# Attention, gated MoE and a second feed-forward on one core: another filler for TensorE and fewer weight conversions at the start

## The chip, the core and the metric

The kernel runs on one core of a Trainium2 chip. The core has a matrix engine (TensorE, PE in the profile, with its weight loads as PEld), three elementwise engines (VectorE or DVE, ScalarE or ACT, GpSimd or POOL) and SyncE (SP), which issues DMA transfers here. Each engine takes its instructions in program order, and semaphores join them. The metric is device time in microseconds (us) of one execution; the clock of TensorE can be granted at 1.2 or at 2.4 GHz.

## What is computed

Three layers follow one another, all in 32-bit floats:

```python
# attention: batch 4, 8 heads, 576 positions, head width 64
scores = q @ k.T / 8 + minimum(cum[j] - cum[i], 0)     # causal, cum = cumsum(max(s, 0))
x = softmax(scores) @ v                                # gathered to 2304 x 512
# gated layer, 512 -> 1536 -> 512
x = (sigmoid(x @ w_gate) * (x @ w_val)) @ w_out
# second layer, 512 -> 2048 -> 512
h = x @ w_in
out = (h - tanh(h)) @ w_out2
```

The weights reach the kernel as 64-bit words (doubles), and the kernel itself turns each block of them into 32-bit floats, and these into a high part (fp32r) and a low part, so that a product of the gated layer is three passes: high times high, low times high, high times low.

## The kernel before

The program is one stream of work per engine, written out in order. Attention runs as steps `i`, one for each pair of a head and a block of 128 query rows. The first 16 heads ("units" `u` below `N32`) do their rows 0 to 255 in two steps each, plain 32-bit products with a contraction of 65 rows; later units use split operands. Steps 0 to 31 are those of the first kind, from step 32 on come the others.

A step issues, in this order: the scaled scores' reduction on DVE (`ttr`, L391), for the step two back the reciprocal of its row sum on DVE and its normalisation on POOL (`norm`, L414), the evacuation of transposes on ACT (`evac`, L441), the exponential on ACT (`exp`, L398), the evacuation of products of the gated layer (`moe_post`, L539 and L542), loads on SP, then on PE the next step's scores (`qk`, L363 and L364), a product group of the gated layer (`moe`, L526 to L530) if one is queued, the transposes of the step two back (`tr`, L428), and at the end of a head the product with the values (`pv`, L459). PE takes them in that order: a transpose that waits for its `norm` holds everything behind it.

Products of the gated layer can start when a batch's x is whole, that is after the eighth head: the first is issued at step 20. Until then (`i < 2 * H + 4`, that is 20 steps) each step issues one idle product, `warm(1)`: a 128x128 identity against 512 columns of zeros (L588). Ahead of the first scores stand `WARM = 9` of the same. All idle products write bank 0, and each waits for the one before.

The conversion of the gated layer's 24 weight blocks is the class `Conversion`. One `tick` moves three blocks on by a stage: ACT writes the high part of block `ticks - 2` (L124), POOL its low part (L114), in `cut` pieces that `low` hands out one at a time, DVE joins the words of block `ticks - 1` (two instructions, L82 and L83), and ACT scales the words of block `ticks` (L78), for which its raw words must have come by DMA. `PRE` ticks stand ahead of step 0; then a step for which `CONV_AT(i)` holds ends with one tick. At the head of a step `cvt.finish` makes further ticks where the products of the step need a block that isn't done. Two ticks before the loop, five by step 14 (`CS`), and one at the end of each step from 15 on: twelve before step 20. After that one tick a step is enough until step 28, whose head forces one more. Nine steps from step 20 on have two product groups each, the next six have one.

The next batch's products start at step 36, and from there PE has work behind work until the end of the program.

## Time and profile before

| | us |
|---|---|
| median of three runs | 1082.97 |
| lowest, highest | 1082.9, 1084.63 |
| profiled execution | 1082.91 |
| its span, first to last instruction | 1080.9 |
| PE busy in the span | 1049.8 (97%) |

The span is read first, then the 40 slices: PE stands at 9 tenths or more in nearly all of them, and the slices under 9 lie in the first 110 us. A timeline of that part by engine then shows who holds PE there, the table of stretches shows the busy time and granted clock of each part, and the durations of one kind of product tell the clock's level where the table has no record of it.

### The profile page before, as it was taken

Reading aid. Unit: us, or ns where it says so; the run is one execution under the profiler, and the core shown is the slowest. Engines: PE = TensorE matmul, PEld = TensorE weight load, DVE = VectorE, ACT = ScalarE, POOL = GpSimd, SP = SyncE. Lnnn points to the kernel's source line nnn. Section 1 sums busy time; section 2 is a strip of 40 time slices with the busy share of each in tenths; the row PEclk is TensorE's granted clock in tenths of the full one; section 3 lists DMA queues with packets and bytes.
Section 4 is the critical chain, followed back from the end, with each engine's and each line's share of the span. In section 5 each row is a group of like instructions: output and inputs, shape, how many; then the busy total and the mean of one; then the engine's idle time right before and its main releaser. Section 6 shows DMA issues by size and latency. Waiting matters only on the chain.

```text
span 1080.9 us, 21941 instructions
## 1 busy us (share of the span) xinstructions
PE 1049.8 (97%) x7589; PEld 1018.6 (94%) x7589; DVE 660.8 (61%) x1627; ACT 546.3 (51%) x1288; POOL 464.7 (43%) x612
## 2 busy tenths in 40 slices
PE   8898999999999999999999999999999999999998
PEld 4697999899999999999999999999999999999997
DVE  6765565778677777664545562254444446778876
ACT  6765565667566566653434543344444433333433
POOL 4757454667556666642401220033323412354442
PEclk9898999999999999999999999999999999999999
DMA  7663346657565565515565553245457589535433
GB/s 224 211 224 99 118 133 165 198 153 172 139 181 134 161 169 160 131 42 170 174 200 174 188 157 95 77 134 167 136 200 268 203 285 336 190 106 152 138 96 100
DMA packets 119791, 177.25 MB, mean 164 GB/s; under 512 B 16960, under 2 KB 98368, under 8 KB 118400
## 3 DMA queue, kind: packets, MB, share of 16 engines
q1 hardware_dynamic: 119680, 175.85, 53.4%
q8 instruction: 60, 0.98, 0.4%
q14 instruction: 51, 0.42, 0.1%
HBM read 128.79 MB, written 47.00 MB: 163 GB/s over the span
## 4 chain that ended last, share of the span: by engine, by line
PE 88%; DVE 3%; ACT 2%; DMA 2%; issue 2%; POOL 2%; SPq 0%; DVEq 0%; POOLq 0%; ACTq 0%
PE bank L526 9%; PE bank L527 9%; PE bank L530 9%; PE bank L813 6%; PE bank L816 6%; PE bank L812 6%; PE bank L948 5%; PE bank L947 5%; PE bank L946 5%; PE bank L774 5%; PE bank L467 5%; PE bank L778 5%; PE bank L775 5%; PE bank L428 4%; PE bank L372 2%
## 5 line engine op out<-in xcount | busy, mean ns | idle before, releaser
L948 PE MATMUL bank<-wo,sl 128*128 128x256 f32 x504 | 142.6, 283 | 1.1 <-DVE sl L861 0.8
L946 PE MATMUL bank<-wo,sh 128*128 128x256 f32 x504 | 141.8, 281 | 0.1
L947 PE MATMUL bank<-wo,sh 128*128 128x256 f32 x504 | 141.7, 281 | 0.0
L812 PE MATMUL bank<-yh,big 128*128 128x288 f32 x512 | 139.6, 294 | 0.0
L813 PE MATMUL bank<-yh,big 128*128 128x288 f32 x512 | 139.6, 295 | 0.0
L446 ACT ACTIVATE pth<-bank 128x512 fp32r<-128x512 f32 (+2 forms) x128 | 59.5, 465 | 144.8 <-PE bank L467 86.2
L819 DVE TENSOR_TENSOR th<-bank,th 128x288 f32<-128x288 f32 x128 | 57.5, 456 | 114.1 <-ACT th L818 112.4
L447 DVE TENSOR_TENSOR ptl<-bank,pth 128x512 fp32r<-128x512 f32 (+2 forms) x128 | 66.7, 521 | 67.7 <-PE bank L467 37.5
L818 ACT ACTIVATE th<-bank 128x288 f32<-128x288 f32 x128 | 51.9, 410 | 101.1 <-PE bank L816 98.5
L948 PEld LDWEIGHTS bank<-wo,sl 128*128 128x128 f32 x504 | 95.3, 189 | 2.1 <-DVE sl L861 1.0
L398 ACT ACTIVATE sp<-sp,nm 128x576 f32<-128x576 f32 (+2 forms) x160 | 95.5, 597 | 2.0 <-DVE nm L391 1.8
L813 PEld LDWEIGHTS bank<-yh,big 128*128 128x128 f32 x512 | 96.1, 188 | 0.0
L812 PEld LDWEIGHTS bank<-yh,big 128*128 128x128 f32 x512 | 96.0, 188 | 0.0
L428 PE MATMUL bank<-ident,sp 128*128 128x128 f32 (+1 forms) x480 | 75.2, 265 | 21.0 <-POOL sp L414 10.8
L946 PEld LDWEIGHTS bank<-wo,sh 128*128 128x128 f32 x504 | 95.3, 189 | 0.3 <-ACT sh L859 0.3
L947 PEld LDWEIGHTS bank<-wo,sh 128*128 128x128 f32 x504 | 95.3, 189 | 0.0
L856 POOL TENSOR_TENSOR s<-g 128x256 f32<-128x256 f32 (+1 forms) x40 | 35.4, 885 | 127.3 <-DMA g<-h 97.4
L816 PE MATMUL bank<-yl,big 128*128 128x288 f32 x512 | 88.6, 294 | 0.0
L720 DVE TENSOR_TENSOR gl<-g,gh 128x384 fp32r<-128x384 f32 x72 | 39.9, 557 | 75.9 <-PE bank L778 47.6
L428 PEld LDWEIGHTS bank<-ident,sp 128*128 128x128 f32 (+1 forms) x480 | 51.9, 140 | 35.9 <-POOL sp L414 20.2
L414 POOL TENSOR_SCALAR sp<-sp,r 128x512 f32<-128x512 f32 (+1 forms) x96 | 61.4, 640 | 48.1 <-DVE r L407 35.2
L719 ACT ACTIVATE gh<-g 128x384 fp32r<-128x384 f32 x72 | 37.3, 529 | 80.7 <-PE bank L775 74.8
(374 smaller groups left out, 3210.8 us busy)
## 6 DMA issues: line engine op xcount, KB each, us to landing
h<-th SPq DMA_DIRECT2D x128, 144.0 KB, 1.9
kq<-in_kq SPq DMA_DIRECT2D x32, 448.0 KB, 3.9
raw<-in_wo SPq DMA_DIRECT2D x28, 512.0 KB, 5.0
g<-g SPq DMA_DIRECT2D x72, 192.0 KB, 2.6
g<-h SPq DMA_DIRECT2D x72, 128.0 KB, 2.2
w<-wst SPq DMA_DIRECT2D x5, 1792.0 KB, 6.2
wo<-w SPq DMA_DIRECT2D x5, 1792.0 KB, 9.1
cbc<-cum SPq DMA_DIRECT2D x32, 256.0 KB, 5.5
```

Of the source, the lines that this page charges most:

```text
L398: ACT.activation(out=e["sp"], in_=e["sp"], func=AF.Exp, scale=-1.0, bias=e["m"], accum_out=e["sum"])
L428: PE.transpose(ps[:, j, :], e["sp"][p0:128, c:c + 128], ident[p0:128, p0:128])
L447: DVE.tensor_tensor(out=pl[:, js, o:o + n], in0=e["tr"], in1=ph[:, js, o:o + n].bitcast(F), op=ALU.subtract)
L526: PE.matmul(ps, wh[:, c], xh[:, k], start=(k == 0), stop=False)
L527: PE.matmul(ps, wl[:, c], xh[:, k], start=False, stop=False)
L530: PE.matmul(ps, wh[:, c], xl[:, k], start=False, stop=(k == KD - 1))
L812: PE.matmul(ps, wh[:, c], Y_[blk][k][0], start=(k == 0), stop=False)
L813: PE.matmul(ps, wl[:, c], Y_[blk][k][0], start=False, stop=False)
L816: PE.matmul(ps, wh[:, c], Y_[blk][k][1], start=False, stop=(k == KD - 1))
L946: PE.matmul(o, sh[:, g, c], w[:, 0, f], start=(p == 0 and t == 0), stop=False)
L947: PE.matmul(o, sh[:, g, c], w[:, 1, f], start=False, stop=False)
L948: PE.matmul(o, sl[:, g, c], w[:, 0, f], start=False, stop=(p == MP - 1 and t == nt - 1))
```

## The change

- The idle products take other data: `some`, 128 rows by 256 columns in bf16, made from a running sum of 0.37 (a memset and a scan on DVE, one conversion on ACT), both as weights (its first 128 columns) and as moving data. They have 256 columns in place of 512. Twenty stand ahead of the first scores in place of nine, two stand in each step in place of one.
- One conversion tick ahead of step 0 in place of two; then ticks after steps 0, 3, 6, 10, 14, and one a step from 18 on, in place of 1, 4, 7, 10, 13 and one a step from 15 on. Eight ticks stand before step 20 in place of twelve.
- From step 19 on the low part of a block is one POOL instruction of 512 columns in place of two of 256.
- The DMA of the second block's raw words is issued ahead of the first two of v.

```diff
-WARM = 9
-PRE = 2
-CS = (1, 4, 7, 10, 13)
+WARM = 20
+PRE = 1
+CS = (0, 3, 6, 10, 14)
 def CONV_AT(i):
-    return i in CS or i > 14
+    return i in CS or i > 17
...
+    some = consts[:, 1024:1152].bitcast(BF)
     DVE.memset(zt, 0.0)
+    DVE.memset(consts[:, 512:768], 0.37)
+    DVE.tensor_tensor_scan(out=consts[:, 768:1024], data0=consts[:, 512:768], data1=consts[:, 512:768], initial=0.0,
+                           op0=ALU.add, op1=ALU.add)
+    ACT.activation(out=some, in_=consts[:, 768:1024], func=AF.Copy)
...
+    cvt.load(2)
     load_vc(0)
     load_vc(1)
-    cvt.load(2)
...
-            PE.matmul(bank(0, [128, 512]), identb, zero.bitcast(BF), start=True, stop=True)
+            PE.matmul(bank(0, [128, 256]), some[:, 0:128], some, start=True, stop=True)
...
-            warm(1)
+            warm(2)
...
+        if i == 2 * H + 3:
+            cvt.cut = 1
         if CONV_AT(i):
             cvt.tick()
```

On ACT, at the start of the program, before. The scalings of raw words (`raw`) are ticks, the two rows on `sp` are the exponentials of steps 0 and 1:

```order
L567 ACT_TABLE_LOAD
L567 ACTIVATE consts<-ident 128x128
L568 ACTIVATE consts<-consts 128x128
L78 ACTIVATE tmp<-raw 128x512
L78 ACTIVATE tmp<-raw 128x512
L398 ACTIVATE sp,sum<-sp,nm 128x128
```

And after:

```order
L565 ACT_TABLE_LOAD
L565 ACTIVATE consts<-consts 128x256
L572 ACTIVATE consts<-ident 128x128
L573 ACTIVATE consts<-consts 128x128
L78 ACTIVATE tmp<-raw 128x512
L398 ACTIVATE sp,sum<-sp,nm 128x128
L78 ACTIVATE tmp<-raw 128x512
```

The second block's scaling now stands behind the first exponential, and one conversion to bf16 (`consts<-consts 128x256`, the filler) stands ahead of all.

On ACT from the exponential of step 23 to that of step 24, before (`th` evacuates a product group, each `w..h` is the high part of one block):

```order
L398 ACTIVATE sp_939,sum<-sp_939,nm 128x256
L539 ACTIVATE th<-bank_900 128x256
L480 ACTIVATE xh<-bank_915 64x256
L124 ACTIVATE w16h<-tmp 128x512
L78 ACTIVATE tmp<-raw 128x512
L441 ACTIVATE p_947<-bank_973 128x256
L398 ACTIVATE sp,sum<-sp,nm 128x128
```

And after:

```order
L398 ACTIVATE sp_965,sum<-sp_965,nm 128x256
L539 ACTIVATE th<-bank_926 128x256
L480 ACTIVATE xh<-bank_941 64x256
L124 ACTIVATE w14h<-tmp 128x512
L78 ACTIVATE tmp<-raw 128x512
L124 ACTIVATE w05h<-tmp 128x512
L78 ACTIVATE tmp<-raw 128x512
L441 ACTIVATE p_972<-bank_998 128x256
L398 ACTIVATE sp,sum<-sp,nm 128x128
```

Two ticks stand one behind the other there, and so they do at five steps, 24 to 28; before, that is so at step 28 alone.

On POOL at steps 28 to 31, before (`kl` and `qs` split the operands of later units, `sp<-sp,r` is the normalisation for which a transpose on PE waits):

```order
L319 TENSOR_TENSOR kl<-kq,kh 128x256
L323 TENSOR_TENSOR qs<-kq,qs 64x256
L114 TENSOR_TENSOR w19l<-tmp,w19h 128x256
L414 TENSOR_SCALAR sp<-sp,r 128x256
L114 TENSOR_TENSOR w19l<-tmp,w19h 128x256
L114 TENSOR_TENSOR w010l<-tmp,w010h 128x256
L414 TENSOR_SCALAR sp<-sp,r 128x128
L114 TENSOR_TENSOR w010l<-tmp,w010h 128x256
```

And after:

```order
L319 TENSOR_TENSOR kl<-kq,kh 128x256
L323 TENSOR_TENSOR qs<-kq,qs 64x256
L114 TENSOR_TENSOR w19l<-tmp,w19h 128x512
L414 TENSOR_SCALAR sp<-sp,r 128x256
L114 TENSOR_TENSOR w010l<-tmp,w010h 128x512
L414 TENSOR_SCALAR sp<-sp,r 128x128
```

Each low part is one instruction, and it stands whole ahead of the next normalisation.

## Rows read from the trace of the kernel before

**Rows 1.** The page: PE's busy time, share and instructions.
```profile
PE 1049.8 (97%) x7589; PEld 1018.6 (94%) x7589; DVE 660.8 (61%) x1627; ACT 546.3 (51%) x1288; POOL 464.7 (43%) x612
```

**Rows 2.** Stretches: us, busy us (instructions) of PE PEld DVE ACT POOL, PEclk, DMA.
```profile
32.00:41.00 9.00, 5.60 (x33) 3.94 (x34) 8.06 (x23) 7.49 (x21) 7.72 (x11) 1.00 0.94 304
41.00:49.00 8.00, 7.58 (x35) 6.37 (x34) 4.78 (x18) 5.50 (x15) 6.03 (x10) 0.57 0.80 252
49.00:80.00 31.00, 31.00 (x251) 30.16 (x250) 21.42 (x62) 20.66 (x57) 17.39 (x26) 1.00 0.63 200
80.00:103.00 23.00, 17.82 (x124) 16.34 (x123) 13.14 (x52) 14.03 (x46) 18.65 (x33) 0.93 0.38 103
```

**Rows 3.** Timeline of PE at the start: start us, us, engine, line, operation.
```profile
2.39 5.73 PE L588 MATMUL bank<-consts 128*128 128x512 bf16 x9 [2.39 <-ACT consts L567]
7.91 0.63 PE L363 MATMUL bank<-kq 65*128 65x128 f32 x2
13.35 0.47 PE L428 MATMUL bank<-ident,sp 128*128 128x128 f32 x1 [0.86 <-POOL sp L414]
17.79 0.39 PE L363 MATMUL bank<-kq 65*128 65x128 f32 x2
```

**Rows 4.** Timeline of the other engines at the start.
```profile
0.91 0.54 DVE L560 MEMSET zt<- 32x576 f32 x1 [0.91 <-PEq L988]
2.67 0.28 DVE L570 TENSOR_SCALAR sraw<-sraw 32x256 f32<-32x256 f32 x1 [1.22 <-DMA sraw<-in_s]
2.99 0.68 DVE L571 TENSOR_TENSOR_SCAN cumsum<-sraw,zt 32x256 f32<-32x256 f32 x1
10.07 0.66 ACT L78 ACTIVATE tmp<-raw 128x512 f32<-128x512 f32 x1 [4.37 <-DMA raw<-in_wv]
10.63 0.39 ACT L398 ACTIVATE sp<-sp,nm 128x128 f32<-128x128 f32 x1
```

**Rows 5.** Timeline of PE: scores issued at steps 7, 15 and 19.
```profile
20.30 0.39 PE L363 MATMUL bank<-kq 65*128 65x128 f32 x2
...
32.81 0.39 PE L363 MATMUL bank<-kq 65*128 65x128 f32 x2
...
41.43 0.49 PE L363 MATMUL bank<-kq 65*128 65x128 f32 x2
```

**Rows 6.** Timeline of PE: the first product groups of the gated layer.
```profile
44.27 0.56 PE L526 MATMUL bank<-xh,w00h 128*128 128x256 f32 x1
...
46.98 0.41 PE L428 MATMUL bank<-ident,sp 128*128 128x128 f32 x1
...
48.33 0.39 PE L526 MATMUL bank<-xh,w10h 128*128 128x256 f32 x1
...
51.78 0.36 PE L526 MATMUL bank<-xh,w11h 128*128 128x256 f32 x1
...
53.30 0.59 PE L363 MATMUL bank<-kq 65*128 65x256 f32 x2
```

**Rows 7.** Chain that ended last (start us, us, what): scores issued at steps 25, 27.
```profile
65.22 0.22 PE bank L363 x2
...
72.81 0.22 PE bank L363 x2
```

**Rows 8.** Groups by shape, DVE, 0 to 110 us: busy us, mean ns, idle before.
```profile
L82 DVE TENSOR_SCALAR tmp<-tmp 128x512 uint32<-128x512 uint32 x24 | 13.5, 564 | 1.7 <-ACT tmp L78 1.5
L83 DVE SCALAR_TENSOR_TENSOR tmp<-raw,tmp 128x512 uint32<-128x512 uint32 x15 | 12.1, 809 | 0.5
```

**Rows 9.** The same view of POOL, 0 to 110 us: low parts.
```profile
L114 POOL TENSOR_TENSOR w010l<-tmp,w010h 128x256 fp32r<-128x256 f32 x2 | 2.3, 1170 | 0.0
...
L114 POOL TENSOR_TENSOR w011l<-tmp,w011h 128x256 fp32r<-128x256 f32 x2 | 1.5, 733 | 0.0
```

**Rows 10.** Instructions of L114: duration ns min/median/max, in a later stage.
```profile
L114 POOL TENSOR_TENSOR big<-tmp,big x16: 1297/1337/1342, 558.5 to 652.1; 128x512 fp32r<-128x512 f32 x16
```

**Rows 11.** PE's waits, 76 to 103 us: us in total, times, longest.
```profile
PE bank L428 <- POOL sp L414: 2.6, 2, 1.9
```

## The prediction

> **What bounds the kernel now.** I read the page first, then the busy time by stretch, then the timelines of the first 110 us. PE is busy 97% of the span [rows 1], so over most of the program only PE's own work counts, and the change takes none of that away. What it can win lies where PE waits or runs at 1.2 GHz, and that is the start: from 32 to 41 us PE is busy 5.60 of 9.00 us while DVE, ACT and POOL stand at 7.5 to 8.1; from 41 to 49 it is busy, but at a granted clock of 0.57; from 49 to 80 it has no gap; from 80 to 103 it waits again, 17.82 of 23.00, with POOL at 18.65 [rows 2]. After that PE is full to the end, so every microsecond by which that point comes earlier is one off the total. The profiled execution took 1082.91 us, of which 1080.9 are span and 2.0 lie around it; the median of the runs is 1082.97, so I sum against 1082.9. The table of stretches shows 1.00 ahead of 41 us only because no change of the clock had been recorded; the rows tell the level: the first scores' product takes 0.63 us at 7.91 and the same form 0.39 at 17.79 [rows 3]. PE began at the lower level, and nine products of zeros back to back (2.39 to 8.12) did not lift it; it rose only after transposes, scores and value products followed one another from 13.35 on.
>
> **Fewer conversions before step 20.** From the scores issued at step 7 (20.30) to those of step 15 (32.81) are 8 steps with 3 ticks in 12.51 us, 1.56 a step; from there to those of step 19 (41.43) are 4 steps with 4 ticks in 8.62, 2.15 a step [rows 5]. With x for a bare step and t for a tick, x + 3t/8 = 1.56 and x + t = 2.15, so t = 0.95 and x = 1.21. Between the first transpose and the scores of step 19 the old order has ticks at 4, 7, 10, 13 and 15 to 18, the new one at 3, 6, 10, 14 and 18: three fewer, **2.8 us** earlier. Were all of t waiting that would come otherwise, it is 0; the upper end is 4, if the conversions' share of contention goes too. I take the fit, since both pieces lie in one stage at one clock.
>
> **The start.** DVE gets a memset and a scan ahead of its first work on s: 0.3 to 0.54 us (the 576-column memset took 0.54) and 0.68 (the scan of as many columns), so it is done with them between 2.4 and 2.7; s lands at 2.67 [rows 4], so that costs 0 to 0.1. ACT then converts the filler, some 0.4 as its 128-column exponential, and PE starts at about 3.0 in place of 2.39. An idle product of 512 columns takes 0.64 (5.73 / 9), of which 0.43 are columns at 1.2 GHz and 0.21 waiting for the one before; with 256 columns it is 0.43, at 2.4 GHz perhaps 0.27. Twenty take 8.6 us at the lower level, 5.4 at the upper, 7.0 with the change halfway, and the first scores come at 10.0 in place of 7.91 [rows 3]. That looks like 2.1 us lost, but the first exponential stood behind the second block's scaling, which waited 4.37 us for its DMA until 10.07, and ran at 10.63 only [rows 4]. Now that tick is behind it, so the exponential runs about 1 us after the scores, at 11.1, and the first transpose (13.35 now) follows at 13.6 to 14.4, since a join of 1.4 us on DVE still stands ahead of the second reduction [rows 8]. I take **0.7 us lost**, with 1 us won (a quick rise) and 3.4 lost (no rise, below) as the ends. The second raw block goes out ahead of two loads of v, which nothing needs before the first value product, behind the first transpose; with the exponential no longer behind it, the transfer gains nothing beyond this and costs nothing; the scores, exponential and transpose of the first head cover the later v, and were that cover gone, the first value product would wait up to the 4.37 us that ACT waited for the same block [rows 4], once. The second idle product of a step waits for the first: up to 0.21 us in each of 18 steps. Where a transpose waits for POOL anyway it hides; bounds 0 and 3.8, I take **0.4 lost**.
>
> **The clock at step 19 to 20.** It fell about when PE's gaps were largest (rows of 32 to 41) and stayed low to past 48 us. With fewer ticks the gaps shrink, and if it holds, three pieces shorten: the first product group took 2.71 us (44.27 to 46.98) against 1.52 at full clock (51.78 to 53.30), the transpose and value product behind it 1.35 (to 48.33), half of that at twice the clock [rows 6], and from 42 to 44.27 about 0.6 of scores and transposes: 1.2 + 0.7 + 0.6 = **2.5 us won**, 0 if it falls again.
>
> **The deferred ticks.** Steps 24 to 28 have two ticks, where only step 28 had. A step there is 7.59 / 2 = 3.8 us of PE [rows 7]. From 49 to 80 DVE was busy 21.42 of 31.00 [rows 2], 2.6 a step; a further tick adds 0.56 + 0.81 = 1.4 [rows 8], 4.0 in all, just over PE's. ACT stood lower, and POOL with 17.39 gets 1.3 more, 3.5 a step. The cover is almost used up: 0.2 over in five steps, some of it from the slack before: **0.6 lost**, 0 to 3.8.
>
> **Whole low parts.** From step 28 on POOL also splits operands, and PE waits 2.6 us for its normalisations [rows 11]. The five low parts made there cost 1.5 to 2.3 us each in two halves [rows 9], 8.7 together; whole ones cost 1.34 in a later stage [rows 10], 6.7 together. Of the 2.0 that POOL saves about half stands on the path: **1.0 won**, 0 to 2. Against it, a normalisation can stand behind 1.34 in place of 0.73.
>
> **Sum:** 2.8 - 0.7 - 0.4 + 2.5 - 0.6 + 1.0 = 4.6; 1082.9 - 4.6 = **1078.3 us**, with its own range 1075.5 to 1080.8.
>
> **The rivals.** *The filler's data change nothing*: then the clock stays low past the twenty products. They end at 11.6 us; from the first scores to the first transpose PE had 4.6 us of work at that clock (7.91 to 13.35, less 0.86 of waiting [rows 3]), and gets 0.6 more by the doubled products of three steps, so the first transpose comes at 16.8, 3.4 late; a lower clock for longer costs another 0.5, step 19's fall stays. -3.4 - 0.5 - 0.4 + 2.8 - 0.6 + 1.0 = -1.1: 1084.0. For it: zeros back to back looked busy and did nothing, and products of half the width leave the array waiting more. Against it: from 13.35 on it was other data, no denser a row, that came before the rise. The Trainium skill ("TensorE: Matmul & The Clock Gate", Part 1) says that the gate follows how busy PE has been recently, and names no data; by that rule the ramp does no better than the zeros, which is this rival, and the zeros at 2.39 to 8.12, which it would have expected to lift the clock, already disagree with it.
>
> *It rises late, but holds*: only with attention's own products, and the filler between them helps to keep it past step 20. The start loses 3.4, the late 2.5 is won: -3.4 - 0.4 + 2.8 + 2.5 - 0.6 + 1.0 = 1.9, 1081.0.
>
> *The deferred work starves PE, and it gets slower*: the place is steps 24 to 34. If each of the four deferred ticks costs there what it cost at steps 15 to 18, that is 3.8; if in the six steps of one product group the normalisations wait the 0.6 that a whole low part is longer, 3.6 more. 2.8 - 0.7 - 0.4 + 2.5 - 3.8 - 3.6 = -3.2: 1086.1. It decides from about 0.9 us of wait a step. For it, DVE's 4.0 against 3.8; against it, PE had no gap at all from 49 to 80 [rows 2], across the one step with two ticks' start.
>
> **How the numbers follow.** Forecast 0.55; no effect of the data 0.20 (a fourth of it slower than 1085.1); late rise 0.11; starved 0.11; other 0.03. Runs of this kernel tell 0.2%, 2.2 us, from no change. Faster is the forecast and a little of the late rise, 0.58; slower is the starved case and a part of the first rival, 0.15; 0.27 stay within. The range leaves out the starved case and the slowest part of the first rival: 1075.5 to 1084.5.
>
> **What would show it.** Right: the first scores near 10 us with rows of 0.39 rather than 0.63; step 19's scores at about 39; the first product group near 41 with a granted clock of 1.00; no wait on PE in the 30 us behind it; less than 2.6 us of waits for POOL at the switch. Wrong: twenty fillers that last 8.6 us, a clock of 0.5 at the first product group, or PE waits for L414 at steps 24 to 28.

## The result, and the profile after

The changed kernel takes 1089.04 us in the median of six runs (1086.86 to 1091.0), the kernel before 1082.93 in runs on the same chip: a ratio of 1.0055 with a 95% interval of 1.0035 to 1.0075. It is slower by about 6 us. The profiled execution took 1087.62 us, of which 1085.5 are span. Every ratio below is to the kernel before on the same chip; its medians on the chips used lie from 1082.7 to 1083.79, so differences in us between kernels that ran on different chips are rough by about 1 us. One of b_ramp's twelve executions ran in a slow state, at 2600.64 us, and is left out of its median.

The page's line on PE answers [rows 1]: the same 97%, and 2.5 us more of busy time.

```profile
PE 1052.3 (97%) x7620; PEld 1017.2 (94%) x7620; DVE 669.5 (62%) x1629; ACT 546.0 (50%) x1289; POOL 463.2 (43%) x593
```

The stretches of [rows 2] in the changed kernel (us, then busy us of PE, PEld, DVE, ACT and POOL, the granted clock, the DMA share, GB/s):

```profile
32.00:41.00 9.00, 8.46 (x53) 5.83 (x51) 5.93 (x30) 6.83 (x26) 4.30 (x8) 1.00 0.54 149
41.00:49.00 8.00, 6.21 (x43) 5.09 (x43) 5.96 (x19) 6.58 (x20) 5.47 (x8) 1.00 0.86 277
49.00:80.00 31.00, 27.87 (x221) 26.41 (x220) 26.38 (x57) 20.89 (x52) 18.51 (x19) 1.00 0.73 237
80.00:103.00 23.00, 18.10 (x126) 16.61 (x126) 15.84 (x51) 14.97 (x46) 18.99 (x26) 0.93 0.47 132
```

Two things turned round. From 32 to 41 us PE went from 5.60 busy to 8.46, and the clock at 41 to 49 from 0.57 to 1.00: that is what the change was written for, though a part of the 8.46 are the doubled idle products. But from 49 to 80, where PE had been busy without a gap, it is now busy 27.87 of 31, and DVE's busy time rose from 21.42 to 26.38.

The start of PE's timeline answers [rows 3] (start us, us, engine, line, operation):

```profile
2.96 8.50 PE L593 MATMUL bank<-consts 128*128 128x256 bf16 x20 [2.96 <-ACT consts L565]
11.25 0.70 PE L363 MATMUL bank<-kq 65*128 65x128 f32 x2
...
11.85 1.17 PE L363 MATMUL bank<-kq 65*128 65x256 f32 x2
...
16.41 0.42 PE L428 MATMUL bank<-ident,sp 128*128 128x128 f32 x1
...
21.16 0.39 PE L363 MATMUL bank<-kq 65*128 65x128 f32 x2
```

Twenty idle products take 8.50 us, 0.425 each; the scores behind them take 0.70, so the clock is still at 1.2 GHz, and it is at 2.4 only by 21.16 (0.39). The first transpose is at 16.41 where it was at 13.35.

PE's waits from 45 to 80 us (us in total, times, longest), of which the kernel before had none; the first of them, behind the first product group; and DVE's two joining instructions by shape, 0 to 110 us, which answer [rows 8]:

```profile
PE bank L428 <- POOL sp L414: 4.7, 4, 1.6
```

```profile
47.06 0.33 PE L428 MATMUL bank<-ident,sp 128*128 128x128 f32 x1 [1.59 <-POOL sp L414]
```

```profile
L83 DVE SCALAR_TENSOR_TENSOR tmp<-raw,tmp 128x512 uint32<-128x512 uint32 x15 | 16.2, 1078 | 0.5
L82 DVE TENSOR_SCALAR tmp<-tmp 128x512 uint32<-128x512 uint32 x24 | 13.6, 568 | 0.2
```

The second join went from 809 to 1078 ns in the mean, with nothing changed in the instruction.

**A ledger.** Five marks on PE's timeline cut the first 110 us into pieces: the first transpose (L428), the first product group of the gated layer (L526 with `w00h`), its seventeenth (`w08h`, at step 28) and its twentieth (`w19h`), and the first value product with split operands (L467). All numbers are starts and differences of starts in us, one profiled execution of each kernel; the kernels below the second line are the experiments.

| kernel | first transpose | to `w00h` | `w00h` to `w08h` | to `w19h` | to L467 | L467 at |
|---|---|---|---|---|---|---|
| before | 13.35 | 30.92 | 32.27 | 6.16 | 19.27 | 101.97 |
| after | 16.41 | 27.40 | 36.03 | 8.41 | 19.31 | 107.56 |
| a_warm9 | 11.85 | 27.98 | 36.02 | 8.42 | 19.31 | 103.58 |
| a_warm9_one | 10.41 | 27.42 | 35.89 | 8.41 | 19.32 | 101.45 |
| a_dense | 10.82 | 26.40 | 35.90 | 8.40 | 20.76 | 102.28 |
| x_dve | 16.41 | 27.91 | 33.25 | 7.29 | 21.46 | 106.32 |
| x_pool | 16.41 | 28.17 | 32.18 | 6.16 | 17.64 | 100.56 |
| b_ticks | 12.29 | 26.35 | 35.37 | 7.32 | 19.79 | 101.12 |
| b_cut1 | 13.52 | 31.32 | 32.82 | 6.58 | 19.51 | 103.75 |
| b_load | 12.56 | 30.97 | 31.16 | 6.16 | 19.15 | 100.00 |
| t_dense | 12.19 | 25.81 | 35.37 | 7.33 | 19.81 | 100.51 |
| t_dense_six | 12.28 | 26.86 | 33.64 | 7.35 | 19.79 | 99.92 |
| t_ramp_load | 12.08 | 26.89 | 33.61 | 7.36 | 19.78 | 99.72 |

Before against after: +3.06 at the start, -3.52 on the way to the first group, +3.76 and +2.25 behind it, +0.04 to L467: 5.59 us, which is the loss. So two questions were open: what the start lost, and why 6.0 us went at steps 20 to 34.

### The profile page after: what moved, and what is told of

Same layout as the page of the kernel before. It is cut to its first block, busy times and chain, and to the rows that moved or that the text cites. A ratio compares the mean times of both kernels' runs of the same rounds, so it can differ in the third digit from the quotient of the medians.

```text
span 1085.5 us, 21993 instructions
## 1 busy us (share of the span) xinstructions
PE 1052.3 (97%) x7620; PEld 1017.2 (94%) x7620; DVE 669.5 (62%) x1629; ACT 546.0 (50%) x1289; POOL 463.2 (43%) x593
## 4 chain that ended last, share of the span: by engine, by line
PE 87%; DVE 5%; issue 2%; DMA 2%; POOL 2%; ACT 1%; SPq 1%; DVEq 0%; POOLq 0%; ACTq 0%
PE bank L526 8%; PE bank L527 8%; PE bank L530 8%; PE bank L820 6%; PE bank L823 6%; PE bank L819 6%; PE bank L955 5%; PE bank L954 5%; PE bank L953 5%; PE bank L467 5%; PE bank L781 5%; PE bank L782 5%; PE bank L785 5%; PE bank L428 4%; PE bank L372 2%
## 5 line engine op out<-in xcount | busy, mean ns | idle before, releaser
L428 PE MATMUL bank<-ident,sp 128*128 128x128 f32 (+1 forms) x480 | 74.8, 264 | 21.1 <-POOL sp L414 8.8
L863 POOL TENSOR_TENSOR s<-g 128x256 f32<-128x256 f32 (+1 forms) x40 | 38.7, 967 | 125.2 <-DMA g<-h 89.1
L428 PEld LDWEIGHTS bank<-ident,sp 128*128 128x128 f32 (+1 forms) x480 | 51.5, 140 | 39.3 <-POOL sp L414 22.1
L414 POOL TENSOR_SCALAR sp<-sp,r 128x512 f32<-128x512 f32 (+1 forms) x96 | 61.1, 637 | 61.7 <-DVE r L407 50.5
```

The lines of the kernel that those rows point to most:

```text
L428: PE.transpose(ps[:, j, :], e["sp"][p0:128, c:c + 128], ident[p0:128, p0:128])
```

## The experiments

### The idle products at the start and in the steps

```
-WARM = 20
+WARM = 9
```

> The changed kernel with nine idle products ahead of the first scores in place of twenty. In the changed kernel's trace the twenty last 8.3 us, all at the lower clock, and the first transpose starts at 16.41 against 13.35 before. Theory (the twenty products are the loss of the start): the first scores at about 6.6 us, the first transpose 2.5 to 3.5 earlier, the total near 1085.5 to 1086.5. Rival (the clock needs them and rises later with fewer): the early transposes come sooner but the rise comes as much later, and the total stays within 1 us of 1089.

Measured: 1085.95 us, ratio 1.0028 [1.0019, 1.0038], 3.1 us less than the changed kernel. The first transpose is at 11.85, 4.56 us earlier, and the ledger from there on is that of the changed kernel but for 0.58 us more on the way to the first group. So the eleven products more were a plain delay. Both kernels have the low clock until 17 to 21 us, so they bought next to nothing. Of the 4.56 us, 3.98 are left at L467 and 3.1 in the medians; where the rest went is not shown.

Then the second product of each step, with nine at the start:

```
-            warm(2)
+            warm(1)
```

> The changed kernel with nine idle products at the start and one, not two, per step. Theory (the second idle product is dear: with nine at the start a pair of steps takes 6.05 us at 19.1 to 31.2 with PE never waiting, against 5.86 with one and waits in the kernel that has the new schedule alone): a pair of steps at 5.85 to 5.9, first product group at 38.3 to 38.8 instead of 39.8, and 1 to 1.6 us off the 1085.95 of the nine, 1084.3 to 1085. Rival (all that is won before step 20 is given back at 24 to 34): waits of 45-80 us grow by what the start wins, 1085.5 to 1086.5.

Measured: 1082.94, ratio 1.0003 [0.9993, 1.0013]. The theory had the sign, but the size is above what either expected: 3.0 us off the nine. Of it 1.44 lie ahead of the first transpose (11.85 to 10.41: three steps whose second product took 0.43 at the low clock, 1.3 us) and 0.56 on the way to the first group. The rest came later in the execution, or is the spread of the runs: at L467 2.1 are left. With this kernel the whole loss is gone, and with the next one as well, by another way: the idle products of the changed kernel, their number and width kept, into one accumulation, so that none waits for the one ahead.

```
-        for _ in range(n):
-            PE.matmul(bank(0, [128, 256]), some[:, 0:128], some, start=True, stop=True)
+        ps = bank(0, [128, 256])
+        for k in range(n):
+            PE.matmul(ps, some[:, 0:128], some, start=(k == 0), stop=(k == n - 1))
```

> The changed kernel, its idle products (twenty at the start, two per step) made into one accumulation each, so that none waits for the one ahead. Theory (spacing kept the clock low): the twenty end 2 to 4 us earlier than at 11.25 and run at 0.21 or less each, first scores with rows of 0.4 or so, the clock at its upper level by 8 us, median 1085.5 to 1087.5. Rival (256 columns of a product are too few whatever the spacing): all of them at the lower level, first scores after 7.3 with rows of 0.6.

Measured: 1082.69, ratio 0.9998 [0.9987, 1.0009], 6.35 us less than the changed kernel and more than the theory gave. Its PE at the start, and behind it PE's idle time ahead of the idle products of the changed kernel, at the start and in the steps (L593: us and times, by what ended it; "issue" is time in which the profile shows nothing that the engine waited for; the same view of a_dense has no such row):

```profile
2.96 4.45 PE L594 MATMUL bank<-consts 128*128 128x256 bf16 x20 [2.96 <-ACT consts L565]
7.20 0.61 PE L363 MATMUL bank<-kq 65*128 65x128 f32 x2
...
7.70 0.65 PE L363 MATMUL bank<-kq 65*128 65x256 f32 x2
...
8.46 0.39 PE L363 MATMUL bank<-kq 65*128 65x128 f32 x2
```

```profile
its engine sat idle before it (us, times) until:
  issue: 6.6, 21
```

Twenty products take 4.45 us instead of 8.50, 0.22 each, which is what the 256 columns take at 1.2 GHz; so the other half of 0.425 was waiting. The twenty and the first scores (0.61) still ran at the lower level, as the rival had it, but right behind them the clock rises: the second scores, of 256 columns, take 0.65 at 7.70, where the same form took 1.17 in the changed kernel. The first transpose comes 5.6 us earlier, and the two pieces behind the first group keep their lengths.

### What lifted the clock: the data or the spacing

The data alone: the ramp of the change with nine products of 512 columns, one per step, each still in a write of its own.

```
+    some = consts[:, 512:768].bitcast(BF)
+    DVE.memset(consts[:, 512:768], 0.37)
+    DVE.tensor_tensor_scan(out=consts[:, 768:1024], data0=consts[:, 512:768], data1=consts[:, 512:768], initial=0.0,
+                           op0=ALU.add, op1=ALU.add)
+    for c in (0, 256):
+        ACT.activation(out=some[:, c:c + 256], in_=consts[:, 768:1024], func=AF.Copy)
...
-            PE.matmul(bank(0, [128, 512]), identb, zero.bitcast(BF), start=True, stop=True)
+            PE.matmul(bank(0, [128, 512]), some[:, 0:128], some, start=True, stop=True)
```

> The kernel before with other data alone in its idle products: the ramp, 512 columns of it, nine products ahead of the first scores and one a step, as many and as wide as before. Theory (nonzero data count for the clock, at this spacing, in the mix with attention's products but not in the lone products at the start): rows at 1.2 GHz until 14 to 18 us, but no fall at step 19, the first product group at full clock, total 1080 to 1081.5. Rival (data never count): rows and fall as before, 1082 to 1083.5, plus about 0.5 for the later start of the filler. Second rival (data count in lone products too): rows at 2.4 GHz before 9 us.

Measured: 1083.22, ratio 0.9999 [0.9988, 1.0010]. The nine take what nine products of zeros took, and the clock stays low as long; later, the first product group runs at full clock (0.36), as the theory had it, and the transpose behind it waits:

```profile
3.26 5.70 PE L594 MATMUL bank<-consts 128*128 128x512 bf16 x9 [3.26 <-ACT consts L566]
8.76 0.63 PE L363 MATMUL bank<-kq 65*128 65x128 f32 x2
...
17.95 0.46 PE L363 MATMUL bank<-kq 65*128 65x128 f32 x2
...
43.86 0.36 PE L526 MATMUL bank<-xh,w00h 128*128 128x256 f32 x1
...
46.96 0.33 PE L428 MATMUL bank<-ident,sp 128*128 128x128 f32 x1 [1.42 <-POOL sp L414]
```

That is no mark of the data. Of the kernels with the old schedule, b_dense_zero below holds the clock at 41 to 49 us too (1.00), with zeros, while it fell with zeros in the kernel before (0.57), b_cut1 (0.62) and b_load (0.82), and with the ramp in b_dense_ramp (0.79). And the held clock is worth little there: in the kernel before the transpose behind the group came at 46.98 without a wait [rows 6], here at 46.96 with one of 1.42 us for its normalisation. From `w00h` to the second group (`w10h`) are 4.06 us in the kernel before, 3.84 here and 3.85 in b_dense_zero.

The same ramp, thirteen products into one accumulation:

```
-WARM = 9
+WARM = 13
...
-            PE.matmul(bank(0, [128, 512]), some[:, 0:128], some, start=True, stop=True)
+        ps = bank(0, [128, 512])
...
+            PE.matmul(ps, some[:, 0:128], some, start=(k == 0), stop=(k == n - 1))
```

> The kernel before with 13 products of the 512-column ramp ahead of the first scores, all into one accumulation, so that none waits for the one before; one a step as before. Theory (it was the spacing that kept the lone products from lifting the clock, 0.21 us of waiting in 0.64): start to start 0.43 us at first and 0.21 before the last of them; the first scores at 2.4 GHz; total 1079 to 1081. Rival (spacing isn't it): all 13 at 0.43, rise with attention's products, total 1081 to 1083.5.

```profile
3.26 4.27 PE L595 MATMUL bank<-consts 128*128 128x512 bf16 x13 [3.26 <-ACT consts L566]
7.36 0.39 PE L363 MATMUL bank<-kq 65*128 65x128 f32 x2
...
13.36 0.47 PE L428 MATMUL bank<-ident,sp 128*128 128x128 f32 x1 [3.59 <-POOL sp L414]
13.62 0.63 PE L363 MATMUL bank<-kq 65*128 65x128 f32 x2
```

Thirteen take less than nine did, and the first scores run at 2.4 GHz 7.4 us into the program. It is worth nothing: 1082.79, ratio 1.0003 [0.9991, 1.0015]. The first exponential still stands behind the second block's scaling (10.64, as in [rows 4]), so PE waits 3.59 us for the first normalisation, and behind that wait the clock is low again (0.63).

And zeros in place of the ramp, thirteen into one accumulation:

```
-WARM = 9
+WARM = 13
...
-            PE.matmul(bank(0, [128, 512]), identb, zero.bitcast(BF), start=True, stop=True)
...
+            PE.matmul(ps, identb, zero.bitcast(BF), start=(k == 0), stop=(k == n - 1))
```

> The kernel before, its nine zero products each into a buffer of its own made thirteen zero products into one accumulation, so that none waits for the one ahead. Theory (the spacing kept the clock low, the data do nothing): the products speed up within the row as the thirteen of the ramp did (4.3 us, some at 0.2), first scores at about 7.4 with rows of 0.39. Rival (the ramp's data count too): all thirteen at 0.43, 5.6 us, first scores at about 8.6 with rows of 0.6.

```profile
2.39 5.73 PE L589 MATMUL bank<-consts 128*128 128x512 bf16 x13 [2.39 <-ACT consts L567]
7.91 0.44 PE L363 MATMUL bank<-kq 65*128 65x128 f32 x2
```

One run, 1083.24. (The nine of the kernel before all wrote bank 0, each as a write of its own.) The thirteen took longer than the ramp's, and yet the first scores run at 0.44 and the next of that form at 0.39: zeros lift the clock too. Where within the thirteen it rises differs from one execution to the next (4.27 to 5.73 us in the six kernels that have them). So for the rise it was the spacing. Idle products that are each a write of their own into the same bank are spaced (the profile shows the gaps only as "issue"), in one accumulation they are not; and a spaced row, though the timeline shows it as one busy piece of 5.7 or 8.5 us, left the clock where it was. The Trainium skill ("TensorE: Matmul & The Clock Gate", Part 1) ties the gate to how busy PE has been recently and names no data, and on the data these runs agree with it, as far as the rise goes.

### What goes at steps 20 to 34

Of the change only the schedule of conversions, on the kernel before:

```
-PRE = 2
-CS = (1, 4, 7, 10, 13)
+PRE = 1
+CS = (0, 3, 6, 10, 14)
...
-    return i in CS or i > 14
+    return i in CS or i > 17
```

> The kernel before with only the conversion schedule of the change (one tick ahead of step 0, then after 0, 3, 6, 10, 14 and from 18 on). Theory (deferring is a gain as long as low parts come in halves and the filler stays): 2 to 3 us won before step 20, at most 1 lost at steps 24 to 28, total 1080 to 1082. Rival (the deferred ticks cost more later than they save): PE waits for normalisations at steps 24 to 28 by 3 us or more, total 1084 to 1086.

Measured: 1082.51, ratio 1.0004 [0.9992, 1.0017]. The first group comes at 38.64 instead of 44.27, 5.6 us earlier and at full clock. Of that 0.85 is left at L467, because the piece from `w00h` to `w08h` grew by 3.10, the next by 1.16 and the last by 0.52. The total meets neither side, the waits meet the rival. PE's waits from 45 to 80 us:

```profile
PE bank L428 <- POOL sp L414: 4.1, 4, 1.3
```

The whole low parts alone, on the kernel before:

```
+        if i == 2 * H + 3:
+            cvt.cut = 1
```

> The kernel before with only whole low parts from step 19 on. Theory (whole low parts hold DVE back even with one tick a step): L83 rises to 1.6 us where it meets one, PE waits at step 20 and at the switch, total 1 to 3 us higher, 1084 to 1086. Rival (they matter only where two ticks stand in a step, and POOL saves time at the switch): 1082 to 1083.

Measured: 1084.91, ratio 1.0015 [1.0003, 1.0027]: a loss of 1.6 us, 0.3 to 2.9 by the interval, as the theory had it. The ledger has +0.55 and +0.42 behind the first group. And taken back in the changed kernel:

```
-        if i == 2 * H + 3:
-            cvt.cut = 1
```

> The changed kernel with each low part in two halves throughout, as before. Theory (a whole low part on POOL holds DVE's joins back: L83 took up to 1.67 us beside it, 1.1 at most beside a half): L83 at most 1.11, PE's waits for normalisations between 45 and 80 us fall from 4.7 to under 2, the total 3 to 4 us lower, near 1085.5. Rival (it is the two ticks in a step alone, cut or not): waits of 4 us or more remain and the total stays at 1088 to 1089.5.

Measured: 1089.06, ratio 1.0060 [1.0038, 1.0081], no different from the changed kernel, and PE's waits from 45 to 80 us are still 4.2. So the theory that the whole low parts are the loss fell; they are a small part of it: the two pieces behind the first group are 0.58 and 1.08 shorter (35.45 and 7.33). (Its profiled execution, with a granted clock of 0.66 from 100 to 110 us, was one of its longest, 1092.01, so its pieces behind 90 us say little.)

What DVE and POOL do to one another shows in the changed kernel's timelines, POOL and then DVE:

```profile
67.67 1.79 POOL L114 TENSOR_TENSOR w16l<-tmp,w16h 128x512 fp32r<-128x512 f32 x1 [0.51 <-ACT w16h L124]
69.41 1.48 POOL L114 TENSOR_TENSOR w07l<-tmp,w07h 128x512 fp32r<-128x512 f32 x1
```

```profile
67.62 0.69 DVE L83 SCALAR_TENSOR_TENSOR tmp<-rawx,tmp 128x512 uint32<-128x512 uint32 x1
68.23 1.51 DVE L82 TENSOR_SCALAR tmp<-tmp 128x512 uint32<-128x512 uint32 x1
69.77 1.67 DVE L83 SCALAR_TENSOR_TENSOR tmp<-raw,tmp 128x512 uint32<-128x512 uint32 x1
71.36 0.28 DVE L391 CUSTOM_DVE_ANT_0 sp<-bank,consts 128x128 f32<-128x128 f32 x1
```

The joins, 0.42 and 0.69 alone, take 1.51 and 1.67 beside two low parts, and the mask and reduction for the next step (L391) comes at 71.36. POOL is drawn out too: the low part of 1.79 started 0.05 us behind a join, where one takes 1.34 in a later stage [rows 10]. PE's four waits from 45 to 80 us end with these normalisations on POOL (L414):

```profile
46.62 0.39 POOL L414 TENSOR_SCALAR sp<-sp,r 128x128 f32<-128x128 f32 x1 [1.32 <-DVE r L407]
...
66.68 0.48 POOL L414 TENSOR_SCALAR sp<-sp,r 128x256 f32<-128x256 f32 x1
...
72.08 0.37 POOL L414 TENSOR_SCALAR sp<-sp,r 128x128 f32<-128x128 f32 x1 [1.19 <-DVE r L407]
...
77.12 0.48 POOL L414 TENSOR_SCALAR sp<-sp,r 128x256 f32<-128x256 f32 x1
```

Two of them (PE's waits of 1.59 and 1.47) come when POOL has stood idle for DVE's reciprocal (L407), which is issued behind the joins. The other two (0.70 and 0.96) come straight behind a low part on POOL itself. Is it the sum of DVE's work, or POOL's subtractions that hold it? Two kernels leave work out, each in one place. In the first, from the ninth block on, DVE joins 64 of the 512 columns, so the other words stay as they were:

```
...
-                words_join(self.tmp[i - 1], self.raw.pop(i - 1))
+                words_join(self.tmp[i - 1], self.raw.pop(i - 1), self.late == 2 and i - 1 >= 8)
```

> The changed kernel with DVE's two joining instructions cut to 64 of 512 columns for all blocks from the ninth on; their words are not joined, all else is as in the changed kernel. It leaves about 1.1 to 3 us of DVE's work out of each two-tick step. Theory (DVE's joins, drawn out beside POOL, are what PE waits for at steps 24 to 28): PE's waits for normalisations from 45 to 80 us fall from 4.7 to under 1.5, total 4 to 6 lower, 1083 to 1085. Rival (POOL or ACT is the bound there): waits of 3 or more, total 1087 to 1089.

Measured: 1086.28, ratio 1.0033 [1.0019, 1.0048], 2.8 us off with nearly all the joining gone. PE's waits from 45 to 80 us fell from 4.7 to 2.2; waits and total lie between the theory and the rival. A join of 64 columns, DVE and POOL:

```profile
63.74 1.26 DVE L85 SCALAR_TENSOR_TENSOR tmp<-rawx,tmp 128x64 uint32<-128x64 uint32 x1
...
66.84 0.22 DVE L85 SCALAR_TENSOR_TENSOR tmp<-rawx,tmp 128x64 uint32<-128x64 uint32 x1
```

```profile
63.62 1.30 POOL L116 TENSOR_TENSOR w06l<-tmp,w06h 128x512 fp32r<-128x512 f32 x1
```

It takes 0.22 us alone and 1.26 beside a low part of 1.30: here it ends when that ends, within 0.1 us. In the second kernel POOL subtracts, from the ninth block on, 128 of the 512 columns, and PE takes these four times:

```
-                for c in range(0, 512, w):
+                for c in range(0, 128 if self.late == 2 and i - 2 >= 8 else 512, w):
...
-            PE.matmul(ps, wl[:, c], xh[:, k], start=False, stop=False)
+            PE.matmul(ps, wl[:, 0:128] if 2 * m + which >= 8 else wl[:, c], xh[:, k], start=False, stop=False)
```

> The changed kernel with POOL's low parts cut to 128 of 512 columns for all blocks from the ninth on (the products take those columns four times, so PE's work stays); the other low columns are not made. Theory (POOL acts through DVE: with short low parts the joins go back to 0.43 and 0.69 us): L83 at 0.7 nearly everywhere, waits from 45 to 80 us under 1.5, and the waits at the switch shorter by 2 or more; total 1082 to 1084.5. Rival (the two joins of a step are too long by themselves): waits of 3 or more from 45 to 80, total 1086 to 1088.

```profile
49.00:80.00 31.00, 31.00 (x252) 30.16 (x251) 24.42 (x70) 25.22 (x65) 14.62 (x23) 1.00 0.83 266
```

Measured: 1081.65, ratio 0.9990 [0.9979, 1.0001], 7.4 us less than the changed kernel, with its late start kept. PE is busy 31.00 of 31 from 49 to 80 again, and the two pieces behind the first group are those of the kernel before, 32.18 and 6.16. The one wait left from 45 to 80 us, 1.6, comes at 47.84, where the low parts are still whole. The second join (L83), from 40 to 110 us, is 858 and 772 ns in the mean of its two forms, where the changed kernel has 1161 and 1032. POOL's low parts, by themselves and through the joins that they hold, are what the deferred conversions run into. The Trainium skill ("SBUF — State Buffer", "SBUF: two separate sides") says that DVE and GpSimd share a pair of ports, which the one that starts first holds for the whole of its instruction, and that a DVE instruction with two inputs in SBUF stands while a GpSimd instruction that reads SBUF holds it; the 1.26 us of the 64 columns agrees.

If so, the subtraction might go to DVE:

```
-                POOL.tensor_tensor(out=o, in0=x, in1=y, op=ALU.subtract)
+                (DVE if self.late == 2 else POOL).tensor_tensor(out=o, in0=x, in1=y, op=ALU.subtract)
```

> The kernel before with the new schedule of conversions, and the low parts of the first conversion subtracted on DVE instead of POOL. Theory (a POOL subtraction of 1.3 us holds DVE's own instruction beside it for about 1.0, which is why the time won by step 20 is given back at steps 24 to 34): 0.72 us more DVE work for each block (two halves of 0.36) takes the place of some 1.0 us of standing, and POOL is free for the norms; the waits of 45-80 us fall from 4.1 to 1 to 2 us, and the median to 1079 to 1081. Rival (DVE's sum of work is what counts): DVE then has about 0.7 us a block more, waits stay at 4 us or grow, 1082.5 to 1085.

> The kernel before with the low parts of the first conversion subtracted on DVE instead of POOL, nothing else. Theory (POOL's subtraction is dear where PE waits for the norms, and before did not wait at steps 20 to 28): little at 45-80 us, the waits of 2.6 us at 76-103 go to about 1, 1081 to 1083. Rival (DVE's sum counts): DVE's joins push the masks and reciprocals back, 1084 to 1086.

Both are slower, beyond what either rival gave: 1092.33, ratio 1.0085 [1.0065, 1.0105], and 1094.62, ratio 1.0103 [1.0084, 1.0123]. Of the theory the holding stands, and the remedy falls. The joins of t_dvelow, by shape from 8 to 80 us, have their bare lengths, with no low part on POOL; but a block's subtraction takes DVE 0.83 us, and ahead of it DVE now stands for ACT's high part, 8.6 us in all from 8 to 80 us, with the masks and reciprocals of the steps behind it. The joins, and the two largest of the subtractions' waits:

```profile
L83 DVE SCALAR_TENSOR_TENSOR tmp<-raw,tmp 128x512 uint32<-128x512 uint32 x12 | 8.3, 692 | 0.4
L82 DVE TENSOR_SCALAR tmp<-tmp 128x512 uint32<-128x512 uint32 x18 | 7.6, 420 | 0.0
L114 DVE TENSOR_TENSOR w00l<-tmp,w00h 128x256 fp32r<-128x256 f32 x2 | 0.8, 416 | 1.3 <-ACT w00h L124 1.3
L114 DVE TENSOR_TENSOR w01l<-tmp,w01h 128x256 fp32r<-128x256 f32 x2 | 0.8, 416 | 1.2 <-ACT w01h L124 1.2
```

In t_dvelow the first group came at 46.18 (38.64 in b_ticks), and PE's waits grew to 5.4 us at 45 to 80. In b_dvelow, with ticks packed ahead of step 20, the first group came at 54.46.

### The loads, and a version that puts the parts together

```
-    load_vc(0)
-    load_vc(1)
     cvt.load(2)
+    load_vc(0)
+    load_vc(1)
```

> The kernel before with the second raw block loaded ahead of the first two blocks of v, nothing else. Theory (the order of these loads costs nothing, the second block is scaled after the first masks anyway): same first transpose within 0.3 us of 13.35, 1082 to 1083.5. Rival (the first values come late, or the second scaling earlier stands ahead of the first exponential): first transpose over 0.5 us later or earlier, and 0.5 to 1.5 us of time either way.

Measured: 1081.43, ratio 0.9988 [0.9975, 1.0002], not told apart from the kernel before. The theory of no effect missed the start: ACT scales the second block at 8.85 instead of 10.07, so the first exponential, which stands behind it in this kernel, runs at 9.42 instead of 10.63, and the first transpose comes 0.8 us earlier.

```profile
8.85 0.67 ACT L78 ACTIVATE tmp<-raw 128x512 f32<-128x512 f32 x1 [2.97 <-DMA raw<-in_wv]
9.42 0.39 ACT L398 ACTIVATE sp<-sp,nm 128x128 f32<-128x128 f32 x1
```

The schedule with thirteen unspaced ramp products, and the same with a sixth conversion ahead of step 18:

```
-WARM = 9
-PRE = 2
-CS = (1, 4, 7, 10, 13)
+WARM = 13
+PRE = 1
+CS = (0, 3, 6, 10, 14)
...
+        ps = bank(0, [128, 512])
...
+            PE.matmul(ps, some[:, 0:128], some, start=(k == 0), stop=(k == n - 1))
```

> The kernel before with the new schedule of conversions, and thirteen ramp products into one accumulation at the start. Theory (what is won by step 20 is given back at steps 24 to 34, since those go at the pace of the conversions): first scores at 7.4 with rows of 0.39, first transpose at 11 to 12, first product group at 37 to 39, and yet waits of 4 to 6 us at 45-80 and a median of 1081.5 to 1083. Rival (an early clock keeps its gain once the exponential no longer stands behind the second raw block): 1078 to 1081.

```
-CS = (0, 3, 6, 10, 14)
+CS = (0, 3, 6, 9, 12, 15)
```

> The kernel before with thirteen unspaced ramp products and the new schedule, but six conversions ahead of step 18 instead of five (at 0, 3, 6, 9, 12, 15). Theory (DVE and POOL have room in steps 0 to 18, where PE waits 3.1 us, and none in steps 20 to 34, where it waits 4.1): first product group within 0.5 us of 38.0, waits at 45-80 us 3 or less, 1080.3 to 1081.7. Rival (each conversion ahead of step 18 costs what one behind it does): 1081.5 to 1083.

Measured: 1081.92, ratio 0.9989 [0.9979, 0.9999], and 1081.62, ratio 0.9990 [0.9979, 1.0001]. The first is a gain of a tenth of a per cent, most of what the start won being given back, as the theory said. In the second, one conversion moved ahead of step 18 makes the way to the first group 1.05 longer and the piece behind it 1.73 shorter; the times of the two can't be told apart. The first group, at 39.14, missed the theory's 38.0 by more than its 0.5; the waits, 2.6, met it.

Last, t_dense_six with the second raw block ahead of v as well, and the same with zeros in place of the ramp:

```
-    load_vc(0)
-    load_vc(1)
     cvt.load(2)
+    load_vc(0)
+    load_vc(1)
```

> The kernel before with thirteen unspaced ramp products at the start, one per step, six conversions ahead of step 18, low parts in halves, and the second raw block ahead of v. Theory (the parts that cost nothing alone add up once the idle products are not spaced): first scores at 8.8, 1079.5 to 1081.5, faster than the kernel before by 0.1 to 0.3%. Rival (what is won before step 20 is given back at steps 24 to 34): 1082 to 1083.

```
...
-            PE.matmul(ps, some[:, 0:128], some, start=(k == 0), stop=(k == n - 1))
+            PE.matmul(ps, identb, zero.bitcast(BF), start=(k == 0), stop=(k == n - 1))
```

> The same with thirteen unspaced products of zeros, which need no ramp and start at 2.39 instead of 3.26. Theory (the data do nothing, the start of the products counts): first scores at 7.9 with rows of 0.44 or less, 0 to 0.9 us less than with the ramp. Rival (the ramp's data hold the clock in later steps): the clock falls between steps 2 and 20 here and not there, and the time is 1 us or more above the ramp's.

Measured: with the ramp 1080.81, ratio 0.9974 [0.9961, 0.9986], the one kernel that is clearly faster than the kernel before, by 0.14 to 0.39%; with zeros 1081.7, ratio 0.9991 [0.9980, 1.0003]. The zeros start PE earlier, but in the profiled execution their clock was low again for two steps and the ramp's was not, and the first group came at the same time, 39.06 against 38.97. PE's timeline with the ramp, and with zeros:

```profile
8.67 0.39 PE L363 MATMUL bank<-kq 65*128 65x128 f32 x2
...
15.77 0.39 PE L363 MATMUL bank<-kq 65*128 65x128 f32 x2
```

```profile
7.54 0.39 PE L363 MATMUL bank<-kq 65*128 65x128 f32 x2
...
15.43 0.63 PE L363 MATMUL bank<-kq 65*128 65x128 f32 x2
```

PE waited 1.0 us twice ahead of these rows in both. Whether the ramp's data help to hold the clock stays open. For it: behind two waits of about 1.0 us the ramp kept the clock in all four kernels that have such waits with it (a_dense, t_dense, t_dense_six, t_ramp_load), and the zeros lost it in the one that has them with zeros. Against it: these are single executions, the two intervals overlap, and b_dense_ramp lost the clock with the ramp, behind a longer wait.

## Why the prediction was wrong

The second product group (`w10h`, at 48.33 before and 47.81 after) divides the ledger by the prediction's terms, in us won:

| piece | predicted | came |
|---|---|---|
| to the first transpose | -0.7 | -3.06 |
| from there to `w00h` | 2.8 - 0.4, and 0.6 of the clock's 2.5 | 3.52 |
| `w00h` to `w10h` | the clock's other 1.9 | 0.06 |
| `w10h` to L467 | -0.6 + 1.0 | -6.11 |

So the largest miss is the deferred work behind `w10h`, then the start, then the clock's worth.

- **The start (0.7 lost): wrong, 3.06.** The step that failed is "7.0 with the change halfway". The clock did not rise within the twenty, nor in the eight microseconds behind them (a transpose at 19.82 still takes 0.42). The working had the reason in hand, 0.43 of columns and 0.21 of waiting in a product of 512; it even said of the first rival that products of half the width leave the array waiting more, and then went by the data all the same. The rival's 16.8 for the first transpose was met by 16.41. That the exponential gains by standing ahead of the second scaling was right: it starts 1.30 us behind the first scores (12.55), where it was 2.72. With nine products at the start and one a step (a_warm9_one) the first transpose comes 2.94 us earlier than before; the second product of three steps then costs 1.44 and the eleven products more cost 4.56.
- **The second idle product (0.4 lost): too small.** The 3.0 of a_warm9_one are the price of the whole second product, columns and waiting; the term was for its waiting alone, so half of that, 1.5, is an estimate by the halves of 0.425, within the bounds of 0 to 3.8. Up to 0.21 in each step was reckoned as hidden behind waits; in the three steps ahead of the first transpose nothing hides it, and there, at the low clock, a second product cost 0.43 each, its columns included.
- **Fewer conversions (2.8 won): right, and more.** In b_ticks, where neither the filler nor its number is changed, the way from the first transpose to the first group shrank by 4.57 us, where 2.8 and the clock's 0.6 were forecast; a part of it is that the clock was up by 15.35 us there (a transpose of 0.27) and not at 17.79. The changed kernel got 3.52 of this, with its second products in the way.
- **The clock at step 19 (2.5 won): it held, but was worth about 0.7.** The step that failed is that the product group, and the transpose and value product behind it, shorten by 1.2 and 0.7 with the clock. The group does run at full clock, but then the transpose behind it waits 1.59 us for its normalisation, and from `w00h` to `w10h` 4.00 us pass in place of 4.06. b_ramp and b_dense_zero, with the old schedule and a clock that held, gained 0.2 there. At the low clock PE's slower work had covered that wait.
- **The deferred ticks (0.6 lost): wrong, 4.3.** In b_ticks the two pieces behind the first group grew by 3.10 and 1.16; counted from `w10h` on it is 5.0. The failed step is the rate of "4.0 in all, just over PE's": it added mean lengths of the joins, 0.56 and 0.81 [rows 8], and took them for lengths that stay. With more low parts on POOL beside them they grow. Both figures lie past the bound of 3.8 that the prediction gave.
- **Whole low parts (1.0 won): wrong sign.** On the kernel before they cost 1.6 us (b_cut1). The ledger of a_dense against b_ticks, which have whole parts and halves on one schedule, has 0.53 and 1.08 more behind the first group, and a_cut2 got 0.58 and 1.08 back. POOL saves time by whole parts, as reckoned [rows 9, 10], but PE pays for what the normalisation and the joins stand behind them, as the prediction's last sentence on them had it.
- **The rivals were priced one at a time, and two came true together.** The clock rose late and held, and the deferred work starved PE. The late rise with the starved case's -3.8 and -3.6 in place of -0.6 and +1.0 is -3.4 - 0.4 + 2.8 + 2.5 - 3.8 - 3.6 = -5.9, that is 1088.8, against 1089.04 measured. That it comes so close is in part luck: the clock's 2.5 in it is too high by 1.8 and the starved case's 7.4 by 1.3. No case held both, so the range ended at 1084.5.

As a sum of what was measured up to L467: -3.06 + 3.52 - 3.76 - 2.25 - 0.04 = -5.59. Not settled is how the deferred ticks' 4.3 us divides between POOL's own queue and the held joins. In the changed kernel's one trace 3.06 of the 4.7 us of PE's waits came through DVE's reciprocals and 1.66 straight behind POOL's low parts. x_dve shortened the piece from `w00h` to `w08h` by 2.78 us and the next by 1.12, x_pool took 3.85 and 2.25 off, but cutting POOL's work frees DVE too.

## What to carry to other kernels

Idle products that are to lift TensorE's clock must not wait for one another: put them into one accumulation, and look at the length of a known row behind them, not at the busy share. What a higher clock gives back in a stretch is not the whole of the shortened work, if PE then reaches a wait that the slower work had covered; look at the next wait before pricing it. Moving work out of one stage wins only what the stage that receives it has to spare on every engine, and the length of an instruction there has to be read beside the company that it will have, since DVE's joins and POOL's subtractions stretched one another here. When two rivals don't exclude each other, price them together as well.

## What was not expected of the hardware

A DVE instruction of 64 columns took 1.26 us beside a POOL subtraction of 1.30, and 0.22 alone: its length there was that of the other engine's instruction, not its own. Thirteen unspaced idle products of 512 columns, zeros or a ramp, had the clock up by the first or second scores, whereas nine spaced ones of 5.7 us and twenty of 8.50 had not.
